# A new hand-fixed issue order, with landing constants and a port rule in its planner, for an adaLN block of linear attention and SwiGLU

## The chip, the cores and the metric

One core of one Trainium2 chip runs the kernel. The metric is the device time of one execution in microseconds (us), the median of the runs shown; lower is better. The core has five instruction streams: TensorE (PE, matrix products; its weight loads are listed apart as PEld and overlap), VectorE (DVE), ScalarE (ACT), GpSimd (POOL) and SyncE (SP, which here issues nearly all DMAs). Each engine takes its instructions strictly in the order in which the program lists them, and waits on semaphores for results of the others.

## The reference

```python
# x: 2048 x 512; H = 32 heads of 16; F = 1376; c: 1 x 512
mod = silu(c) @ w_mod                      # sa, ca, ga, sb, cb, gb, 512 each
h = layernorm(x) * (1 + ca) + sa
q, k, v = h @ wqkv                         # per head
phi(t) = concat(softmax(t @ w_phi), softmax(-t @ w_phi))
kv = sum_s phi(k)^T v ;  z = sum_s phi(k)
o = phi(q) kv / (phi(q) z + 1e-6)
x = x + ga * (o @ wo)
h = layernorm(x) * (1 + cb) + sb
x = x + gb * ((silu(h @ w_gate) * (h @ w_up)) @ w_down)
```

## The kernel before

The 2048 tokens are 16 tiles of 128, in four chunks of four. The work is not issued as it is written down. Every step (one matmul group, one evacuation, one DMA) is registered with `pl.op` together with what it reads and writes, and, where several engines can do it, with one alternative for each (L390 to L400 for a normalization: DVE, ACT or POOL). The table `ORDER` (L46) then fixes the order: entry `x` is operation `x // 4` in the order of registration, done by alternative `x % 4`. `Plan.run` (L168) walks the table once, gives each operation a planned start from fixed durations and constants, and emits the instructions sorted by that start. Two steps of one engine therefore come in the order in which the table has them, whatever the constants say. The constants decide three things beside the order: which buffer slot a tile gets, how steps of different engines interleave in the listing, and how many filler matmuls (`fill`, L1037 on, instructions at L1054, on a tile of ones) go in front of a PE step whose planned start lies after the end of the one before. Before the first kv step the filler takes the whole planned gap, later about 85% of it, and none after 90 us of the plan.

An alternative marked `DVE*` is a VectorE step that the planner believes to take the SBUF port that VectorE and GpSimd share. Nothing in the program enforces that: there is no semaphore for it, it only moves planned starts.

Stages, in the order of time, with the lines at which they show in the profile:

- Loads, all on SP's queue (L289): x of chunk 0, `Wk2`, `w_phi`, the two modulation parts of `w_mod` in three pieces, x of chunk 1 in two, then x of chunk 2, `Wq2`, `wv_sb`, x of chunk 3.
- `w_phi` is folded into the key and query weights (`fold_phi`): four blocks i, each transposed (PE at L519 for the keys, DMA at L292 for the queries), evacuated (L523), multiplied with a block-diagonal matrix `BD` (L502, product at L530) and evacuated again (L533, L534).
- Modulation: `silu(c)` times `w_mod`, four groups k (PE L473), evacuated as `modA` (DVE L478).
- First layernorm (`first_norm`): bn_stats (L348), bn_aggr (L349), rstd (POOL L381 and L382, or ACT L377 and L378), negative mean (L384), normalization (L392, L396 or L398). Transposes of the result are PE's for tiles 0 to 5 (L563, L414), evacuated with the modulation (L566, L567, L422), and DMAs for tiles 6 to 15 (L577), modulated at L585 to L589.
- `k_tile` i: K (PE L619), its two exponentials (ACT L634), V (PE L623), sums (DVE L640), their reciprocals (ACT L644, L645), `va` (DVE L650), two POOL steps (L648, L657). `kv_tile` (PE L663) accumulates. `q_tile` (PE L686, ACT L690, DVE L694, POOL or DVE L701, DMA L705) is the same for the queries. These share six PSUM banks (`one_ps`).
- `gate`, `mod_cols` and `spread_gate` make the other modulation vectors from two further loads of `w_mod`.
- `prepare`: attention output (PE L824), transposed (L843 or a DMA, L847), projected (PE L857), added to x, second layernorm, transposed again (L414 or a DMA, L871).
- Feed-forward: `ffn_gu` (PE L909; ACT L916; DVE L919, or ACT L923 and POOL L925), `ffn_tail` (PE L955), `ffn_down` (PE L987; DVE L997 and DVE or POOL L1001, or DVE L993), stores (L1007). Only the last token tile is stored in three pieces of columns: 0 to 256, 256 to 384 and 384 to 512.

## Time and profile before

| | us |
|---|---|
| median of 3 runs | 199.46 (199.35 to 200.03) |
| span of the profiled execution, first to last instruction | 197.6 |
| PE busy in the span | 192.9 |
| DVE, ACT, POOL busy | 139.9, 111.6, 119.5 |
| mean granted PE clock of the span | 1.000, so the 2.4 GHz level |

The record gives the profiled execution's span, not a device time of its own; the median of the runs is 1.9 us longer than the span. In the rows below a timeline row is "start, duration of the group, engine, line, operation, out<-in, count"; a group of xN instructions is merged, and its duration runs from the first start to the last end, so that steps that overlap in the pipeline are closer together than their single durations. A row of five windows gives for each engine the busy time and the number of instructions in that stretch. A DMA row ends with the median time from issue to landing.

### The profile page before, as it was taken

The page shows a single profiled execution, that of the slowest core. Times are in us where ns is not written, and L with a number is a line of the kernel's source. Part 1 is how long each engine was busy: PE and PEld are TensorE (multiplying, and loading weights), DVE is VectorE, ACT ScalarE, POOL GpSimd, SP SyncE. Part 2 cuts the span into 40 slices and gives each one's busy share as a digit, 9 for nine tenths or more (in the row PEclk, how much of TensorE's full clock was granted, in tenths as well). Part 3 has the DMA queues.
Part 4 walks back from the last instruction along what each step waited for, and adds up shares of the span by engine and source line. Part 5 has one row for each costly group of instructions (what it writes and reads, how often), then busy time and mean ns, then how long its engine had stood idle before and what let it go on. Part 6 is the DMA issues. An engine that isn't in the chain of part 4 may idle for free.

```text
span 197.6 us, 4084 instructions
## 1 busy us (share of the span) xinstructions
PE 192.9 (98%) x1495; PEld 108.4 (55%) x1495; DVE 139.9 (71%) x272; ACT 111.6 (56%) x252; POOL 119.5 (60%) x198
## 2 busy tenths in 40 slices
PE   7999999999999999999999999999999999999993
PEld 2765555555754776886575554454445444444452
DVE  5999999999999999989868689384122421181653
ACT  2699999999769982665263625435723411235200
POOL 1459999999996669656757979406761004065310
PEclk9999999999999999999999999999999999999999
DMA  6997994999928672835377515400340020100202
GB/s 210 370 373 116 168 316 162 213 181 389 324 53 170 117 138 42 157 65 102 77 113 135 109 36 87 100 0 0 80 98 25 0 63 17 56 15 27 80 29 79
DMA packets 51142, 24.17 MB, mean 122 GB/s; under 512 B 42449, under 2 KB 47922, under 8 KB 51122
## 3 DMA queue, kind: packets, MB, share of 16 engines
q1 hardware_dynamic: 50976, 23.88, 50.0%
q8 instruction: 11, 0.18, 0.3%
q14 instruction: 9, 0.07, 0.1%
q10 hardware_dynamic: 146, 0.03, 0.1%
HBM read 11.58 MB, written 2.10 MB: 69 GB/s over the span
## 4 chain that ended last, share of the span: by engine, by line
PE 98%; DVE 0%; issue 0%
PE one_ps L909 35%; PE one_ps L987 19%; PE one_ps L857 7%; PE one_ps L623 7%; PE one_ps L619 7%; PE one_ps L686 7%; PE kv_ps L1054 4%; PE one_ps L955 3%; PE kv_ps L663 2%; PE kv_ps L824 2%; PE one_ps L530 1%; PE one_ps L473 1%; PE one_ps L414 1%; PE one_ps L519 0%; PE one_ps L722 0%; DVE ones L296 0%
## 5 line engine op out<-in xcount | busy, mean ns | idle before, releaser
L909 PE MATMUL one_ps<-hT,wgu_sb 128*128 128x512 bf16 (+2 forms) x480 | 75.7, 308 | 0.0
L909 PEld LDWEIGHTS <-wgu_sb 128*128 128x128 bf16 x480 | 40.3, 98 | 27.7
L916 ACT ACTIVATE sg<-one_ps 128x512 bf16<-128x512 f32 (+1 forms) x41 | 23.7, 588 | 41.8 <-PE one_ps L909 29.9
L925 POOL TENSOR_TENSOR gu<-usb,sg 128x512 bf16<-128x512 bf16 x19 | 21.8, 1151 | 39.7 <-ACT usb L923 19.9
L987 PE MATMUL one_ps<-wd_sb,gu 128*128 128x512 bf16 (+1 forms) x160 | 37.7, 372 | 0.0
L919 DVE TENSOR_TENSOR gu<-one_ps,sg 128x512 bf16<-128x512 f32 (+1 forms) x22 | 14.3, 652 | 21.1 <-PE one_ps L909 19.0
L987 PEld LDWEIGHTS <-gu 128*128 128x128 bf16 x180 | 16.6, 98 | 16.7
L997 DVE TENSOR_TENSOR fg<-one_ps,gab 128x512 bf16<-128x512 f32 (+1 forms) x16 | 10.5, 669 | 19.6 <-PE one_ps L987 19.4
L348 DVE BATCH_NORM_STATS2 st<-x_c 128x6 f32<-128x512 bf16 x32 | 21.0, 679 | 0.1
L640 DVE TENSOR_REDUCE S<-e 128x64 f32<-128x1024 bf16 x16 | 19.1, 1207 | 0.2
L694 DVE TENSOR_REDUCE Sq<-eq 128x64 f32<-128x1024 bf16 x16 | 19.0, 1201 | 0.0
L923 ACT CAST usb<-one_ps 128x512 bf16<-128x512 f32 x19 | 11.3, 594 | 13.5 <-PE one_ps L909 13.2
L690 ACT ACTIVATE eq<-one_ps 128x512 bf16<-128x512 f32 x32 | 17.3, 644 | 2.2 <-PE one_ps L686 2.2
L634 ACT ACTIVATE e<-one_ps 128x512 bf16<-128x512 f32 x32 | 16.9, 600 | 0.0
L657 POOL TENSOR_TENSOR e<-e,S 128x512 bf16<-128x512 bf16 x16 | 16.8, 1056 | 0.1
L857 PE MATMUL one_ps<-wo_sb,oT 128*128 128x512 bf16 x64 | 16.1, 379 | 0.0
L623 PE MATMUL one_ps<-wv,hT 128*128 128x512 bf16 x64 | 16.1, 379 | 0.0
L619 PE MATMUL one_ps<-wk,hT 128*128 128x512 bf16 x64 | 15.8, 379 | 0.0
L686 PE MATMUL one_ps<-wq,hT 128*128 128x512 bf16 x64 | 15.8, 379 | 0.0
L701 POOL TENSOR_TENSOR eq<-eq,Rq 128x512 bf16<-128x512 bf16 x13 | 14.2, 1096 | 0.5
L860 DVE TENSOR_TENSOR x_c<-x_c,one_ps 128x512 bf16<-128x512 bf16 x16 | 10.6, 674 | 4.5 <-PE one_ps L857 4.4
L880 ACT ACTIVATE hT<-raw,modB 128x256 bf16<-128x256 bf16 x16 | 8.9, 594 | 8.1 <-DMA raw<-xn 8.1
(120 smaller groups left out, 279.8 us busy)
## 6 DMA issues: line engine op xcount, KB each, us to landing
wmod_sb<-in_w_mod_dram SPq DMA_DIRECT2D x2, 1024.0 KB, 8.5
out_dram<-ot SPq DMA_DIRECT2D x15, 128.0 KB, 2.0
x_c<-in_A_x_dram SPq DMA_DIRECT2D x3, 512.0 KB, 6.7
wgu_sb<-in_B_w_up_dram SPq DMA_DIRECT2D x1, 1376.0 KB, 10.2
wgu_sb<-in_B_w_gate_dram SPq DMA_DIRECT2D x1, 1376.0 KB, 13.1
wd_sb<-in_B_w_down_dram SPq DMA_DIRECT2D x1, 1280.0 KB, 6.8
wk<-in_A_wqkv_dram SPq DMA_DIRECT2D x1, 512.0 KB, 4.9
wmod_sb<-in_w_mod_dram SPq DMA_DIRECT2D x1, 512.0 KB, 5.3
```

Of the source, the lines that this page charges most:

```text
L348: pl.op("DVE", r=reads, w=[st6], us=0.6, fn=lambda: nc.vector.bn_stats(st6()[:], src))
L619: nc.tensor.matmul(pk()[:], lhsT=hT[c_i][k][:, cols], rhs=Wk2[:, k, :], start=(k == 0), stop=(k == KD - 1))
L623: nc.tensor.matmul(v()[:], lhsT=hT[c_i][k][:, cols], rhs=wv_sb[:, k, :], start=(k == 0), stop=(k == KD - 1))
L640: pl.op("DVE", r=[e], w=[Ss], us=1.13, fn=lambda: nc.vector.tensor_reduce(Ss()[:].rearrange("p g s h -> p (g s h)"), e()[:].rearrange("p g ...
L686: nc.tensor.matmul(pq()[:], lhsT=hT[c_i][k][:, cols], rhs=Wq2[:, k, :], start=(k == 0), stop=(k == KD - 1))
L690: pl.op("ACT", r=[pq, btab], w=[be[sg]], us=0.48, fn=lambda sg=sg: nc.scalar.activation(eq[:, :, sg].rearrange("p g h f -> p g (h f)"), pq ...
L694: pl.op("DVE", r=be, w=[Sq], us=1.13, fn=lambda: nc.vector.tensor_reduce(Sq()[:].rearrange("p g s h -> p (g s h)"), eq[:].rearrange("p g s ...
L857: nc.tensor.matmul(a()[:], lhsT=oT()[:, j0 + j, :], rhs=wo_sb[:, j, :], start=(j == 0), stop=(j == KD - 1))
L909: nc.tensor.matmul(ps_()[0:fsz, q * n:(q + 1) * n], lhsT=wgu_sb[:, k, i, m * P:m * P + fsz], rhs=h2[k], start=(k == 0), stop=(k == KD - 1))
L916: pl.op("ACT", r=[g, btab], w=[sg], us=0.08 + 0.41 * L / CW, fn=lambda: nc.scalar.activation(sg()[0:fsz, 0:L], g()[0:fsz, 0:L], ACT.Silu))
L925: pl.op("POOL", r=[usb, sg], w=[gu], us=0.17 + 0.98 * L / CW, fn=lambda: nc.gpsimd.tensor_tensor(gu()[0:fsz, 0:L], usb()[0:fsz, 0:L], sg() ...
L987: nc.tensor.matmul(fp()[:], lhsT=b()[0:fsz, c0:c0 + P], rhs=wd_[0:fsz, m, wcs], start=(m == 0), stop=(m == FM - 1))
```

## The change

The table `ORDER` is replaced: the same 995 operations in another order, 59 of them by another engine. Planner constants change: the time that a DMA transpose takes to land after its transfer falls from 1.1 to 0.6, the sizes that stand for the load times of the first twelve loads are set anew, and the rule for `DVE*` becomes one over intervals: a `DVE*` step is no longer put behind all POOL steps that the table lists before it, but only out of the way of the POOL intervals that it would overlap (and POOL steps out of the way of `DVE*` ones). The source order of the loads of x chunk 2, `Wq2`, `wv_sb` and x chunk 3 changes, and with it their operation numbers; in both tables SP issues them in the order x 2, `Wq2`, `wv_sb`, x 3. Of the last tile, the piece of columns 256 to 384 is now stored on ACT's queue and that of 384 to 512 on SP's; the new order also computes 384 to 512 before 256 to 384, so that the piece finished last is on ACT's queue in both kernels.

```diff
 ORDER = [
-    0, 48, 4, 188, 8, 52, 12, 16, 20, 24, 56, 80, 60, 72, 220, 84, 76, 156, 228, 192, 64, 204, 89, 172, 232, 224, 92, 160, 196, 164, 177, 102, 201,
...
+    48, 0, 4, 8, 52, 56, 80, 188, 68, 60, 192, 72, 12, 16, 20, 84, 172, 76, 89, 156, 24, 220, 204, 28, 32, 176, 228, 36, 40, 224, 208, 44, 232,
...
 ]
-    DMA = (1.7, 385e3, 0.5, 0.6, 1.15, 1.1)
+    DMA = (1.7, 385e3, 0.5, 0.6, 1.15, 0.6)
...
+        held = {"POOL": [], "DVE*": []}
...
-            if o.alt[0] == "DVE*":
-                o.start = max(o.start, free["POOL"])
...
+            star = o.alt[0] == "DVE*"
+            if star or o.eng == "POOL":
+                for s, e in held["POOL" if star else "DVE*"][-8:]:
+                    if o.start < e and o.start + o.alt[1] > s:
+                        o.start = e
...
-            if o.alt[0] == "DVE*":
-                free["POOL"] = max(free["POOL"], o.end)
+            if star or o.eng == "POOL":
+                held[o.alt[0]].append((o.start, o.end))
...
-    later(x_ch[0][:], x_v[0], bx[0:4], 400)
-    later(Wk2[:], wqkv_v[:, :, D:2 * D], bwk[0:1], 690)
+    later(x_ch[0][:], x_v[0], bx[0:4], 440)
+    later(Wk2[:], wqkv_v[:, :, D:2 * D], bwk[0:1], 755)
...
-    for k, n, kb in ((0, 2, 770), (2, 1, 280), (3, 1, 280)):
+    for k, n, kb in ((0, 2, 470), (2, 1, 262), (3, 1, 250)):
...
-            on_act = c1 == D and h == 1
+            on_act = c0 == D // 2 and c1 < D
```

Decoded, the first steps of PE stand in this order (k: modulation group; fold i: block i of the key weights, or of the query weights where it says so; T: transposes of normalized tiles; K, V, q: tiles):

| before | after |
|---|---|
| transposes of Wk 2, w_phi, transposes of Wk 0, 3, 1 | transposes of Wk 2, w_phi, transposes of Wk 1, 0, 3 |
| fold 2, fold 0, k 0, fold 1, k 1, fold 3 | k 0, k 1, fold 2, fold 0, fold 1, k 2, k 3 |
| T of tiles 0 and 1 (one of four), k 2, k 3, T of tiles 2 and 3 (half), T of 0 and 1 (three), T of 2 and 3 (half) | T of tiles 0 and 1 (four), fold 3, T of tiles 2 and 3 (both halves) |
| K 0, K 1, K 2, T of 4 and 5 (half), K 3, T (half), V 1, V 0 | K 1 and K 0 (halves in turn), K 2, K 3, V 0, T of 4 and 5, V 1 |
| K 4, V 4, K 5, query folds 1, 0, V 5, query fold 3, V 3, query fold 2, V 2, kv 0, q 0, kv 1, q 2 | query fold 2, V 2, query fold 3, V 3, query fold 1, K 4, query fold 0, K 5, q 3, q 0, kv 0, kv 1, q 2 |

Beside them: DVE takes bn_stats and bn_aggr of tiles 0 and 1 before the statistics of tiles 2 and 3 (before: bn_stats of tile 2 in between), then `BD` after the first negative mean. POOL does the constant masks (L329 to L332) first instead of after three normalizations, and normalizes all of tiles 0 to 3 (before: tiles 1 and 2, with ACT for 0 and DVE for 3) and makes the rstd of chunk 2 (before: ACT). ACT evacuates all four T of tiles 0 and 1 (before: three, DVE one) and fold 3 after them. SP's order becomes: query-weight transposes 2, 1, 3, 0 (before 3, 1, 0, 2); transposes of tiles 6 and 7; the first further load of `w_mod` (before: after those of tiles 8 to 11 and the load of `w_down`); transposes of tiles 8 to 11; the second further load of `w_mod` and `wo`; transposes of tiles 12 to 15; `w_down`, `w_up`, the rest of `w_down`, `w_gate`; and only then the first `pT` (before: the first `pT` ahead of `w_up` and `w_gate`). At the end PE does tiles 14, 15 (0 to 256) and 12 in another interleaving, then tile 13 and the two last pieces, as before.

## Rows read from the trace of the kernel before

**Rows 1.** The page, busy time of each engine in the span:
```profile
PE 192.9 (98%) x1495; PEld 108.4 (55%) x1495; DVE 139.9 (71%) x272; ACT 111.6 (56%) x252; POOL 119.5 (60%) x198
```
**Rows 2.** Timeline of PE, 9.9 to 17 us (columns as told above):
```profile
9.90 0.54 PE L473 MATMUL one_ps<-silucT,wmod_sb 128*128 128x1 bf16 x16
...
11.37 1.54 PE L1054 MATMUL kv_ps<-ones 128*128 128x512 bf16 x7
12.74 2.75 PE L619 MATMUL one_ps<-wk,hT 128*128 128x512 bf16 x12
15.33 0.48 PE L1054 MATMUL kv_ps<-ones 128*128 128x512 bf16 x2
...
16.96 1.89 PE L623 MATMUL one_ps<-wv,hT 128*128 128x512 bf16 x8
```
**Rows 3.** Timeline of PE around two of its later waits:
```profile
46.06 1.03 PE L623 MATMUL one_ps<-wv,hT 128*128 128x512 bf16 x4
47.02 0.17 PE L471 MATMUL one_ps<-zero_one,ones 1*128 1x8 bf16 x1
...
62.56 1.89 PE L686 MATMUL one_ps<-wq,hT 128*128 128x512 bf16 x8
64.44 0.29 PE L414 MATMUL one_ps<-ident_b,xn 128*128 128x128 bf16 x2
```
**Rows 4.** Busy time in stretches: PE, PEld, DVE, ACT, POOL, then clock, DMA share, GB/s:
```profile
25.00:30.00 5.00, 5.00 (x36) 2.42 (x33) 5.00 (x10) 4.90 (x16) 5.00 (x8) 1.00 1.00 334
...
50.00:55.00 5.00, 5.00 (x80) 3.28 (x79) 4.86 (x9) 3.04 (x10) 5.00 (x8) 1.00 0.78 267
```
**Rows 5.** Timeline of DVE, 4 to 10.7 us:
```profile
4.33 1.87 DVE L348 BATCH_NORM_STATS2 st<-x_c 128x6 f32<-128x512 bf16 x3
6.12 0.23 DVE L349 BATCH_NORM_AGGREGATE ln_mv<-st 128x2 f32<-128x6 f32 x2
...
7.01 0.69 DVE L502 TENSOR_TENSOR BD<-one_ps,bm 128x512 bf16<-128x512 f32 x1
...
10.48 0.17 DVE L478 COPY modA<-one_ps 128x8 f32<-128x8 f32 x1 [0.38 <-PE one_ps L473]
```
**Rows 6.** Timeline of POOL and ACT in the first 16 us, and POOL's group at L657:
```profile
6.76 0.72 POOL L382 TENSOR_TENSOR ln_mv<-ln_var,mhalf 128x2 f32<-128x2 f32 x1
...
13.72 1.52 POOL L398 TENSOR_SCALAR xn<-x_c,ln_mv,ln_nmr 128x512 bf16<-128x512 bf16 x2 [0.54 <-DVE ln_nmr L384]
...
10.68 1.68 ACT L566 ACTIVATE hT<-one_ps,modA 128x256 bf16<-128x256 bf16 x3
...
L657 POOL TENSOR_TENSOR e<-e,S 128x512 bf16<-128x512 bf16 x16 | 16.8, 1056 | 0.1
```
**Rows 7.** SP's issues in time, and DMA issues of 0 to 30 us by landing:
```profile
2.19 1.44 SPq L289 DMA_DIRECT2D wmod_sb<-in_w_mod_dram  x3
...
wmod_sb<-in_w_mod_dram SPq DMA_DIRECT2D x2, 256.0 KB, 5.6
...
13.06 5.89 SPq L292 DMA_TRANSPOSE WT<-wq  x4
...
raw<-xn SPq DMA_TRANSPOSE x3, 3.3
```
**Rows 8.** Landing of L292's transposes, and DMA issues of 30 to 44 us:
```profile
DMA to landing us min/median/max: 2.5/2.6/4.2
...
pT<-eq SPq DMA_TRANSPOSE x1, 5.7
```
**Rows 9.** The last matmul, and the last store (issues of 190 us on):
```profile
194.12 0.22 PE L987 MATMUL one_ps<-wdg,gut 96*128 96x128 bf16 x1
...
out_dram<-ot ACTq DMA_DIRECT2D x1, 32.0 KB, 1.9
```
**Rows 10.** Instructions of L1001: count, then ns min/median/max, first and last start:
```profile
L1001 DVE TENSOR_TENSOR ot<-x_c,fg x11: 411/424/1104, 109.3 to 194.0; 128x512 bf16<-128x512 bf16 x11
L1001 POOL TENSOR_TENSOR ot<-x_c,fg x5: 667/1154/1729, 124.6 to 191.0; 128x512 bf16<-128x512 bf16 x4, 128x256 bf16<-128x256 bf16 x1
```

More of the change, by code (lines that the diff above doesn't have):

```diff
@@ L428, in modulate_T @@
               r=[tp, bmod], w=[b[2 * jp + jj] for b in [bdst] + list(also) for jj in range(2)])
-    later(x_ch[0][:], x_v[0], bx[0:4], 400)
-    later(Wk2[:], wqkv_v[:, :, D:2 * D], bwk[0:1], 690)
-    later(wphi_sb[:], A_w_phi.rearrange("h (q t) f -> (h q) (t f)", t=4), [bphi], 70)
-    for k, n, kb in ((0, 2, 770), (2, 1, 280), (3, 1, 280)):
+    later(x_ch[0][:], x_v[0], bx[0:4], 440)
+    later(Wk2[:], wqkv_v[:, :, D:2 * D], bwk[0:1], 755)
+    later(wphi_sb[:], A_w_phi.rearrange("h (q t) f -> (h q) (t f)", t=4), [bphi], 75)
+    for k, n, kb in ((0, 2, 470), (2, 1, 262), (3, 1, 250)):
         later(wmod_sb[:, k:k + n, 0:2 * D], wmod_v[:, k:k + n, 0:2 * D], bm1[k:k + n], kb)
     for t in (0, 2):
-        later(x_ch[1][:, t:t + 2, :], x_v[1][:, t:t + 2, :], bx[TPC + t:TPC + t + 2], 270)
-    later(wv_sb[:], wqkv_v[:, :, 2 * D:3 * D], [bwv], 560)
-    later(Wq2[:], wqkv_v[:, :, 0:D], bwq[0:1], 570)
-    for c_i in (2, 3):
-        later(x_ch[c_i][:], x_v[c_i], bx[c_i * TPC:(c_i + 1) * TPC], 620)
+        later(x_ch[1][:, t:t + 2, :], x_v[1][:, t:t + 2, :], bx[TPC + t:TPC + t + 2], 256)
+    for c_i, kb in ((2, 520), (3, 620)):
+        if c_i == 3:
+            later(Wq2[:], wqkv_v[:, :, 0:D], bwq[0:1], 570)
+            later(wv_sb[:], wqkv_v[:, :, 2 * D:3 * D], [bwv], 550)
+        later(x_ch[c_i][:], x_v[c_i], bx[c_i * TPC:(c_i + 1) * TPC], kb)
     sig = const.tile([P, KD], FP32, name="sig")
```

79 rows, old and new, of the table ORDER are left out of this document.

## The prediction

> **What bounds the kernel now.** I read the busy times first: PE 192.9 of 197.6 us [rows 1]. Some of that is filler, so the next view is PE's timeline, and in it the distance from one start to the next. Twelve K matmuls start at 12.74 and the next group at 15.33 [rows 2]: 2.59 / 12 = 0.216 us each, though one is listed much longer. Smaller ones, from the same timeline of which group 2 shows a part: 0.055 us for 128 columns, 0.025 for a modulation column. Laying these distances along all PE steps of the kernel, those from the first K matmul on sum to 180.0 us. The last starts at 194.12 [rows 9], so 12.74 + 180.0 = 192.8, and only 1.4 us between 12.74 and 194.2 is not work: 0.32 filler at 15.33 [rows 2], 0.10 before 47.02 (46.06 + 4 x 0.216 = 46.92) [rows 3], about 0.15 before 64.44 by the same sum [rows 3], the rest smaller. The change takes no PE work away. It can gain before 12.74, in this 1.4 us, and in the 3.4 us from the last matmul to the end, and lose anywhere else. In the middle that is easy: DVE, ACT and POOL are at 4.90 to 5.00 of 5 us at 25 to 30 us, while ACT has air at 50 to 55 (3.04) [rows 4].
>
> **The start, walked by hand.** I follow the new order with distances of before; from one engine's end to another's start I put 0.1 to 0.2 us (POOL's pow ends 7.48 and DVE and POOL go on within that).
>
> DVE: before, the aggregates of tiles 0 and 1 stand behind a third bn_stats, at 6.12 [rows 5]. Three take 1.87, one 0.68, so they are 0.60 apart; behind two the aggregates end near 5.8. POOL's pow then ends near 6.9 instead of 7.48 (6.76 + 0.72 [rows 6]). Two further bn_stats fit into that wait. The price is `BD`: behind the first negative mean it ends near 7.8 instead of 7.70 [rows 5].
>
> POOL normalizes all four tiles, 0.75 apart (two in 1.52 [rows 6]): from 7.3, tiles 0 and 1 end at 8.8; tiles 2 and 3, whose mean comes at 9.2, at 10.8. The masks that go first cost nothing: POOL is idle then until the statistics come.
>
> `modA`: the third `w_mod` piece is issued last of three that begin at 2.19 and take 1.44, so near 3.2, and lands 5.6 later [rows 7]: 8.8. Before, its products waited at 9.90 [rows 2] behind transposes that waited for normalized tiles, and `modA` came at 10.48 [rows 5]. In the new order they stand behind three folds that end at 8.8; two groups of eight at 0.025 end at 9.2, and `modA` comes at 9.4: 1.0 us sooner.
>
> ACT then evacuates four transposes, 0.45 to 0.55 apart (three in 1.68 with a short wait among them [rows 6]), 9.7 to 11.6, and fold 3, to 12.1. PE makes the transposes of tiles 2 and 3 ahead of the first K matmul: 10.9 to 11.36. So K 1 and K 0 start at 11.36; their second halves wait for fold 3, 12.3, and they end at 13.15. Before: 12.74 + 8 x 0.216 = 14.47. **Gain 1.3.**
>
> K 2, K 3, V 0 and the transposes of tiles 4 and 5 follow (normalized by 15.6), V 1 starts at 16.2. Before it starts at 16.96 [rows 2], and V 0 (0.86) is behind it: **gain 1.6**, the filler at 15.33 among it.
>
> Then some is given back. The query-weight transposes wait for the load of `Wq2`, whose place on SP is unchanged: they start at 13.06 in any order [rows 7] and land after 4.2 for the first and 2.5 to 2.6 for later ones [rows 8], that is at 17.2, 17.7, 18.8 and about 20. The new order puts a query fold right behind V 1, at 17.1: wait 0.2. The next, after V 2, takes the transpose issued third: it is wanted at 18.4 and there at 18.9: wait 0.5. q 3 then waits some 0.15 for the evacuation of the last query fold, and starts at 22.3. Counted in PE work done, that is 1.6 - 0.85, **about 0.7 us ahead** of before (the walk's error is some 0.3 either way).
>
> **The middle.** From 22.3 the sum of PE distances puts K 9 at 33.8 and kv 15 at 53.2, where before has it at 53.1 with one query tile (0.86) less done. I take the middle as neutral, 0, by three views:
> - POOL, from its first step of chunk 1 at 14.07: eight normalizations of 0.75, rstd of chunk 2 at 1.2, five small and five large kv steps (1.06 long, 1.02 apart [rows 6]), two part and four full modulations, and a wait of 0.35 for the reciprocal of tile 0: its last modulation for K 9 ends near 33.5. It fits with 0.2 to 0.3 to spare. Moving rstd of chunk 2 to POOL costs it 1.2 us and gives ACT 0.5.
> - The waits before 47.02 and 64.44 may go or come back elsewhere. The first is for the second `w_mod` load, moved ahead by some 13 us, and I count up to -0.1 for it. The transposes at 64.44 now have 5.1 us after the first projection instead of 5.8: between -0.15 and +0.7. Both ends stay in the range.
> - The 59 moved alternatives shift a net three operations to POOL (DVE one less, ACT two less), less than 2 us in 112 to 140 [rows 1]. Behind 100 us these engines have air, and I cost it at 0; without that air it would be at most that 2 us.
>
> **The port rule** costs and gives nothing on PE's path by itself: it emits no wait, it moves planned starts. What it lets happen shows in before: an addition at L1001 takes DVE 424 ns in the median and 1104 at worst, POOL 1154 and 1729 [rows 10]. So overlapped pairs pay 0.6 to 0.7 us each, where neither engine was on PE's path. The Trainium skill, "SBUF — State Buffer", section "SBUF: two separate sides", calls this port pair an exclusive lock that the later instruction waits for in full; the maxima fit that, and each new overlap would then cost the loser at most one POOL instruction. As PE has work queued there, the sum stays as it is.
>
> **The stores**: 0. Renamed pieces, same sizes, same queues in the same order of finishing. The ACT store lands 1.9 us after issue [rows 9]; the end follows PE's last matmul as before, 3.4 us behind.
>
> **Sum.** Span 197.6 - 0.7 = 196.9; with the 1.9 us outside the span, **198.76**.
>
> **The rivals.**
> - *The start is kept, and the old waits go too.* -0.7 with up to another 0.5 off: 198.2 to 198.7. Part of the forecast's case.
> - *The supply engines take the gain back.* At 25 to 30 us all three are full [rows 4]; a PE that is ahead only waits there for a bank or for POOL. If POOL's tail at 33.5 slips by 0.5 to 1, K 9 and kv 4 stand still by 0.3 to 0.8: 199.0 to 199.6, most likely 199.2. For it: the margin of 0.2 to 0.3. Against: ACT's air at 50 to 55 shows that before had some slack to give.
> - *Transposes land late behind a load* (slower). The first further `w_mod` load, 1 MB, goes ahead of the transposes of tiles 8 to 11. Without such a load ahead, three `raw` transposes land in 3.3 us [rows 7]; the first `pT`, issued behind the 512 KB of `wo`, takes 5.7 [rows 8]. If the second transpose of the pair, issued near 24.5, takes 5.7 instead of 3.3, it lands at 30.2 instead of 27.8; POOL stands still before its modulations, and K 9 and kv 4 lose 2.4 - 0.25 = 2.1. That gives 199.46 - 0.7 + 2.1 = 200.9. It decides from a landing after about 28.8. Against: that pair is issued some 4 us after the load, long enough for most of it. The Trainium skill, "DMA: Bandwidth & Descriptors", section "Two DMAs through the same engine are not ordered", says that descriptors of one queue start in order, which would make transposes stand behind any load issued before them; the 5.7 us fits.
> - *The change does nothing at the start*, because filler placed by the plan holds PE until the old time, or ACT's four evacuations (one more than before) do. 199.4.
>
> **How the numbers follow.** Forecast with its better variant 0.49, from 198.0 to 198.9. Supply engines 0.25, 199.0 to 199.6. Late landings 0.18, from 199.7 (half a microsecond late) to 201. Nothing 0.08, 199.3 to 199.6. A measurement tells about 0.3%, 0.6 us, from no change, so faster means under 198.86: nearly all of the first case and a little of the second, 0.49. Same, to 200.06: 0.35. Slower: 0.16. The range 198.0 to 200.2 leaves out the larger part of the late landings and a little below.
>
> **What would show it.** Right: first K matmul at 11.2 to 11.6, fold 3's evacuation the last thing before the second halves, two short PE waits at 17 to 19, q 3 at 22.0 to 22.6, no filler at 15.33, K 9 within 0.3 of 33.8. Supply: gaps of PE at 25 to 50 ended by POOL or ACT evacuations. Late landing: K 9 or kv 4 after 35, POOL idle before L589. Wrong throughout: a first K matmul after 12.3, or PE waits in the feed-forward part after 66 us, where I counted none.

## The result: slower, and where the time lies in the profile after

The changed kernel takes 202.23 us (median of 6, 201.40 to 204.85) against 199.68 (199.35 to 200.26) for the kernel before on the same chip: ratio 1.0124, 95% interval 1.0086 to 1.0162. That is slower by 2.5 us where 0.7 less was forecast, and outside the range. An execution more than 1.5% above the fastest of its kernel counts as slow and stands in the medians and ranges but in no ratio: here that of 204.85 us (without it the median is 201.58), further on two of the four of `wmod_half` (206.39 and the profiled 204.99) and one of `after_delay` (209.61). The profiled execution is one of 203.66 us with a span of 201.8.

Its page, busy time of each engine (before: [rows 1]):

```profile
PE 192.4 (95%) x1469; PEld 107.9 (53%) x1492; DVE 137.8 (68%) x272; ACT 110.9 (55%) x248; POOL 121.4 (60%) x202
```

PE does the same work in a span that is 4.2 us longer. So PE stands still, and the view to read is the list of its waits between 30 and 110 us (waiting line <- what ended the wait: us in total, times, longest us):

```profile
PE kv_ps L669 <- POOL e L663: 1.2, 1, 1.2
PE one_ps L961 <- DVE x_c L866: 0.8, 1, 0.8
PE kv_ps L830 <- DMA pT<-eq: 0.5, 1, 0.5
PE one_ps L961 <- POOL hT L888: 0.3, 1, 0.3
PE kv_ps L830 <- DVE st L353: 0.2, 1, 0.2
```

The same view of the kernel before, in a second profile of it, has no line at all. (This view counts a wait from the modelled end of the matmul before it; by the start-to-start sum of the prediction each is about 0.15 longer, and so I give them from here on.) The lines of the changed kernel stand some 6 below (L663 of before is L669 here, L824 is L830, L955 is L961).

In time, for the profiled execution: 1.36 us before kv 4 at 34.44; 0.38 at 64.34 and 0.31 at 66.89; 0.94 and 0.49 at 79.95 and 80.52; 0.67 at 107.26: 4.15 in all. Before has 0.10 at 47 and 0.33 at 64 and 70. Two names in the list are only the last releaser that the view found: the matmuls at 64.34 use the `pT` issued at 61.01, whose landing is not in the trace, and those at 79.95 and 80.52 use `hT`, which ACT and POOL began to make when the `raw` transpose landed at 79.27.

The start, as a timeline of PE, DVE and POOL in the changed kernel (start, duration, engine, line; the brackets are the idle time ahead and what ended it); before: [rows 2, 5, 6].

```profile
8.64 0.55 PE L479 MATMUL one_ps<-silucT,wmod_sb 128*128 128x1 bf16 x16 [0.33 <-DMA wmod_sb<-in_w_mod_dram]
9.05 0.38 PE L536 MATMUL one_ps<-BD,WT 128*128 128x128 bf16 x4
...
9.78 0.54 PE L479 MATMUL one_ps<-silucT,wmod_sb 128*128 128x1 bf16 x16
...
9.53 0.69 DVE L540 CAST wk<-one_ps 128x512 bf16<-128x512 f32 x1 [1.07 <-ACT ln_mv L383]
10.14 0.15 DVE L389 TENSOR_REDUCE ln_nmr<-ln_mv 128x2 f32<-128x4 f32 x1
...
10.38 1.53 POOL L403 TENSOR_SCALAR xn<-x_c,ln_mv,ln_nmr 128x512 bf16<-128x512 bf16 x2 [1.51 <-DVE ln_nmr L389]
...
11.99 0.61 PE L419 MATMUL one_ps<-ident_b,xn 128*128 128x128 bf16 x8
12.43 3.62 PE L625 MATMUL one_ps<-wk,hT 128*128 128x512 bf16 x16
```

The reader sees one chain without a gap: the first `w_mod` piece lands at 8.59, PE does its products, behind them in PE's order stands a fold, DVE casts the fold, behind that cast in DVE's order stands the negative mean of tiles 2 and 3, POOL normalizes them, PE transposes them, and the first K starts at 12.43. (The bracket of DVE's cast names ACT's L383, but that had ended at 9.17; the fold's products begin at 9.05 and end at 9.43.) The forecast had 11.36.

### The profile page after: what moved, and what is told of

The parts are those of the page before. It is cut to its first block, busy times and chain, and to the rows that moved or that the text cites. A ratio compares the mean times of both kernels' runs of the same rounds, so it can differ in the third digit from the quotient of the medians.

```text
span 201.8 us, 4048 instructions
## 1 busy us (share of the span) xinstructions
PE 192.4 (95%) x1469; PEld 107.9 (53%) x1492; DVE 137.8 (68%) x272; ACT 110.9 (55%) x248; POOL 121.4 (60%) x202
## 4 chain that ended last, share of the span: by engine, by line
PE 63%; DMA 14%; POOL 8%; DVE 5%; ACT 4%; issue 3%; SPq 1%; POOLq 0%; DVEq 0%; ACTq 0%
PE one_ps L915 27%; PE one_ps L993 15%; DMA raw<-xn 8%; PE one_ps L863 4%; PE one_ps L625 3%; PE one_ps L692 3%; PE one_ps L629 3%; DMA wmod_sb<-in_w_mod_dram 3%; POOL xn L403 2%; DMA pT<-eq 2%; PE one_ps L961 2%; ACT e L640 2%; DVE st L353 2%; PE kv_ps L669 2%; POOL ln_rstd L365 1%
## 5 line engine op out<-in xcount | busy, mean ns | idle before, releaser
L915 PE MATMUL one_ps<-hT,wgu_sb 128*128 128x512 bf16 (+2 forms) x474 | 74.2, 307 | 0.3
L993 PE MATMUL one_ps<-wd_sb,gu 128*128 128x512 bf16 (+1 forms) x154 | 36.5, 372 | 0.3
L1003 DVE TENSOR_TENSOR fg<-one_ps,gab 128x512 bf16<-128x512 f32 (+1 forms) x16 | 10.7, 666 | 14.5 <-PE one_ps L993 14.5
L707 POOL TENSOR_TENSOR eq<-eq,Rq 128x512 bf16<-128x512 bf16 x16 | 16.9, 1058 | 0.8
L663 POOL TENSOR_TENSOR e<-e,S 128x512 bf16<-128x512 bf16 x16 | 17.0, 1065 | 0.7
L863 PE MATMUL one_ps<-wo_sb,oT 128*128 128x512 bf16 x62 | 15.5, 379 | 0.1
L629 PE MATMUL one_ps<-wv,hT 128*128 128x512 bf16 x60 | 15.4, 379 | 0.2
L692 PE MATMUL one_ps<-wq,hT 128*128 128x512 bf16 x61 | 15.3, 379 | 0.2
L886 ACT ACTIVATE hT<-raw,modB 128x256 bf16<-128x256 bf16 x15 | 8.3, 594 | 7.5 <-DMA raw<-xn 7.5
```

What stands on the lines that cost most here:

```text
L629: nc.tensor.matmul(v()[:], lhsT=hT[c_i][k][:, cols], rhs=wv_sb[:, k, :], start=(k == 0), stop=(k == KD - 1))
L692: nc.tensor.matmul(pq()[:], lhsT=hT[c_i][k][:, cols], rhs=Wq2[:, k, :], start=(k == 0), stop=(k == KD - 1))
L863: nc.tensor.matmul(a()[:], lhsT=oT()[:, j0 + j, :], rhs=wo_sb[:, j, :], start=(j == 0), stop=(j == KD - 1))
L915: nc.tensor.matmul(ps_()[0:fsz, q * n:(q + 1) * n], lhsT=wgu_sb[:, k, i, m * P:m * P + fsz], rhs=h2[k], start=(k == 0), stop=(k == KD - 1))
L993: nc.tensor.matmul(fp()[:], lhsT=b()[0:fsz, c0:c0 + P], rhs=wd_[0:fsz, m, wcs], start=(m == 0), stop=(m == FM - 1))
```

## The experiments

All times are medians, with the ratio to runs of the kernel before on the same chip (199.5 to 199.8) and its 95% interval behind them. "Waits" are PE's, by start-to-start sums.

**1. Both kernels once more, and each half of the order alone.** `ORDER` is one list, so the first part of one can be joined to the rest of the other: the entries of the first up to about 52 to 55 us, then all others in the sequence of the second (`old` is the table of before, numbered for the changed kernel).

```diff
 # tail_of_before: the changed kernel with
+ORDER = new[:370] + [x for x in old if x // 4 not in {y // 4 for y in new[:370]}]
-            on_act = c0 == D // 2 and c1 < D
+            on_act = c1 == D and h == 1
 # head_of_before: the changed kernel with
+ORDER = old[:350] + [x for x in new if x // 4 not in {y // 4 for y in old[:350]}]
```

> The changed kernel once more, for its spread and for a second trace. Theory 'late transposes' (the w_mod load ahead of the transposes of tiles 8 to 11 makes them land late): those two land 5.5 to 7 us after issue again, PE waits 1.2 to 1.6 us near 33 us, time 201.4 to 203.7 with most of the spread from later waits. Theory 'second half' (the loss is made behind 60 us): the wait near 33 differs from run to run, those behind 60 us stay at 2 to 3 us. Theory 'loads' (the first loads land at other times in each execution, and the new order has no margin for it): the first w_mod piece lands anywhere between 7.5 and 8.6 us, and the time follows it, 201.4 with the early, 203.5 with the late landing.

> The kernel before once more, for a second trace. Theories 'late transposes' and 'second half': 199.4 to 200.2, PE waits of 1.4 us in all from 12.7 us on, first w_mod piece at 7.5 us. Theory 'loads': the first w_mod piece lands at another time than 7.5 (up to 8.6) here too, and the time still stays within 0.5 us of 199.7, since this order plans with later landings.

> The first 370 entries of the new ORDER (the work to about 55 us), then the remaining operations in the old order and with the old engines; constants of the new planner, old queues of the last two stores. Theory 'late transposes': the wait near 33 us stays, time 201 to 202. Theory 'second half': the waits behind 60 us go, time 199.7 to 200.2 (the seam costs up to 0.5). Theory 'loads': as the changed kernel when the first loads are late, 201 to 202.5, else near 200.

> The first 350 entries of the old ORDER (the work to about 52 us), then the remaining operations in the new order; constants of the new planner and new queues of the last two stores. Theory 'late transposes': no wait over 0.5 us before 50 us, time 199.7 to 200.7 (the seam costs up to 0.8). Theory 'second half': the waits behind 60 us stay at 2 us or more, time 201.5 or more. Theory 'loads': near 200.3 in all runs, little spread.

Measured: after_again 202.28 (ratio 1.0141, 1.0120 to 1.0163), before_again 199.46 (0.9996), tail_of_before 201.64 (1.0127, 1.0082 to 1.0172), head_of_before 201.62 (1.0089, 1.0063 to 1.0116). Both halves lose. In the first half (tail_of_before) it is the wait before kv 4, 1.07, and a wait of 1.12 for `wv`, which landed at 16.74 in that execution, not at 14.46 as in the first profile of before. In the second half (head_of_before) it is the waits at 78.3 and 78.9 (0.87, 0.49), behind a `raw` transpose of 72.65 that took 5.0 us, and at 105.5 (0.59), with 0.70 of filler and of waiting for POOL's normalization at the seam. 'Second half' had the waits of the changed kernel's tail stay at 2 to 3 us; in after_again they are 1.69. Its wait near 33, 0.39, is also under the 1.2 to 1.6 of 'late transposes', and its first `w_mod` piece, at 9.28, came later than 'loads' had it. Waits in the second profile of the changed kernel:

```profile
PE kv_ps L830 <- DMA pT<-eq: 0.9, 2, 0.6
PE kv_ps L669 <- POOL e L663: 0.2, 1, 0.2
```

Those at 80 us are not there; the `raw` transpose behind them, issued at 74.24 and 74.10, landed after 5.0 us in the first profile and after 3.2 in the second.

**2. The load ahead of the transposes, halved.**

```diff
-        cols = slice((2 + 2 * i) * D, (4 + 2 * i) * D)
+        cols = slice((2 + i) * D, (3 + 3 * i) * D)
```

> The changed kernel in its own order, with the first of the two further w_mod loads cut to its first 512 columns (0.5 MB in place of 1 MB) and the other 512 put into the second (1.5 MB), so that half as much stands in the queue ahead of the transposes of tiles 8 to 11. 'Late transposes': the transpose issued near 22.5 lands at about 28 in place of 29.4 to 29.7 (5.5 us after issue in place of 6.5 to 7), the wait ahead of kv 4 (0.39 to 1.36 us in three runs) falls to between 0 and 0.3; the second load lands up to 1 us later, which can bring a wait of 0 to 0.7 at the mod B columns near 34.5. Time 0.3 to 1 us below the changed kernel's on the same chip's scale, 200.8 to 202. If the load isn't the cause: landing and wait as before, 201.4 to 203.7.

Measured: 203.80 (201.36 to 206.39), ratio 1.0121 (1.0072 to 1.0171). The DMA issues of 20 to 27 us in the changed kernel (KB each, median us to landing), then what hangs on them, POOL's and PE's timeline:

```profile
wmod_sb<-in_w_mod_dram SPq DMA_DIRECT2D x2, 1024.0 KB, 6.4
raw<-xn SPq DMA_TRANSPOSE x3, 5.5
...
31.08 2.28 POOL L595 TENSOR_SCALAR hT<-raw,modA 128x512 bf16<-128x512 bf16 x3 [1.52 <-DMA raw<-xn]
...
34.44 0.43 PE L669 MATMUL kv_ps<-va,e 128*128 128x68 bf16 x8 [1.20 <-POOL e L663]
```

The two transposes behind the load took 7.0 and 5.5 us and landed at 29.39 and 30.92 (before: 3.3 [rows 7]). POOL stood still 1.52 us for the second, and its kv step came late for PE. With half the load, issues of 20 to 28.5 us and PE's waits of 30 to 60 us:

```profile
wmod_sb<-in_w_mod_dram SPq DMA_DIRECT2D x1, 512.0 KB, 4.1
raw<-xn SPq DMA_TRANSPOSE x3, 3.6
...
PE one_ps L479 <- DMA wmod_sb<-in_w_mod_dram: 0.9, 1, 0.9
```

The first transpose behind the half load took 3.1 us, the second 3.6, and the wait before kv 4 is gone. In its place PE waits 0.94 for the second load, now 1.5 MB: that the load is the cause of the late landings is shown; the time is not won, for the load is wanted elsewhere. (The range was to 0.7 for this second wait; the miss is in its size. The two executions at full clock took 201.36 and 202.61; of the profiled one's clock more is said at the end.)

**3. TensorE's code loads.** In the DMA view a packet of queue 8, kind "instruction", 0.02 MB, comes once per about 128 matmuls (11 of 16 KB in the changed kernel). After the `raw` transpose was issued at 74.24 in the changed kernel such a packet began at 77.05. Issues of 74 to 75 us, and packets of 76.5 to 77.5 (packets, MB, share of 16 engines):

```profile
raw<-xn SPq DMA_TRANSPOSE x1, 5.0
...
q8 instruction: 1, 0.02, 7.2%
```

If these packets hold up transposes, then matmuls added at the very start, where PE only turns over filler, shift the packets against the order and move the late landings with them. So: the same filler in smaller pieces.

```diff
 # after_code32
-                fns.append(lambda n=min(left, CW): f(n))
-                left -= CW
+                fns.append(lambda n=min(left, P): f(n))
+                left -= P
 # after_code77 and before_code78: this, and the first gap filled with
+            if t0 < 3.0:
+                fns += [lambda: nc.tensor.matmul(kv_ps[:, 0, 0:1], lhsT=ones[0:1, 0:P], rhs=ones[0:1, 0:1],
+                                                 start=True, stop=True, skip_group_check=True)] * 60
+                left = 0
```

> The changed kernel with its first filler matmuls cut into pieces of 128 columns: the same columns, some 32 matmuls more before the first K, none elsewhere, so that TensorE's code loads (one 16 KB packet of queue 8 after every 128 or so matmuls) come some 32 matmuls sooner in the program. In the run after_again they start at 27.3, 37.8, 54.0, 68.3, 76.8, 90.5 and 103.2 us. 'Code loads' (a transpose issued 1 to 2.9 us ahead of such a packet lands 4 to 5 us after its issue in place of 3.0 to 3.4): the packets move to about 25, 35, 50.6, 64, 73.4, 87.4 and 100.5; the transpose raw issued at 74.1 lands in 3.0 to 3.4 us whatever the run, the pT ones issued at 88.3 and 101.0 too (4.5 and 4.6 before), and those issued near 62.2, 71.4, 85.2, 97.9 and 99.3 become the late ones. Waits near 80 us 0, near 106 us under 0.2, new ones of up to 1 us behind the late ones. Time 201 to 202.5. 'Second half' (the order itself asks for its transposes too late, wherever the code loads fall): the same late landings at 88.3 and 101.0 and the same wait of 0.6 to 0.8 near 106; time 201.5 to 203.7.

> As after_code32, with some 77 matmuls more before the first K (the first four fillers are replaced by 60 of one column each). 'Code loads': the packets move to about 20, 32, 45, 58.6, 71.2, 83.5 and 95; late become the Wq transposes issued near 17.4 and 18.7, and the pT, gut ones issued near 57.3, 70.1, 81.2 and 82.6; the transposes issued near 35, 74, 88, 98 and 101 land in 3.0 to 3.5 us, and the waits near 80 and 106 us are gone (1.43 and 0.67 in the profile of the changed kernel, 0 and 0.76 in its second one). The transposes of tiles 8 to 11 stay late for the w_mod load. Time 200.5 to 202. 'Second half': waits near 106 stay at 0.6 to 0.8; time 201.5 to 203.7.

> The kernel before with some 78 matmuls more ahead of the first K, as in after_code77. In before_again the packets of queue 8 start at 28.8, 40.8, 53.6, 65.8, 75.4, 88.6 and 101.1 and only the pT transpose issued at 99.9 is late (4.3 us). 'Code loads': the packets move to about 21, 34.4, 48, 58, 69, 81 and 93; late become the transposes issued near 19.1, 33.2, 67.3 (oT, on which TensorE waits 0.2 us at 70.7 already: that wait becomes 0.8 to 2), 78.4 or 79.8, 89.9 and 91.3; time 200 to 201.5, 0.5 to 2 us slower than before although no step of the order is moved. 'Second half': nothing changes but the start, 199.3 to 199.9.

Measured: after_code32 203.49 (1.0205, 1.0162 to 1.0248), after_code77 202.52 (1.0157, 1.0123 to 1.0191), before_code78 200.42 (1.0032, 1.0008 to 1.0055). The first two are above what 'code loads' allowed (202.5 and 202); the landings decide. In after_code77 packets begin near 70.9, 83.1 and 94.6. The `raw` transpose of 74.9 lands after 3.1 us, the `pT` of 67.9 and 80.6 after 4.9 and 5.5; issues of 74 to 76 and of 67.8 to 69.5 us, and PE's waits of 30 to 130:

```profile
raw<-xn SPq DMA_TRANSPOSE x1, 3.1
...
pT<-eq SPq DMA_TRANSPOSE x2, 4.7
...
PE kv_ps L830 <- DMA pT<-eq: 2.1, 2, 1.2
PE kv_ps L830 <- DVE st L353: 0.2, 1, 0.2
```

The waits at 80 and 106 are gone, and new ones stand at 72.9 (1.06) and 86.2 (1.35), each behind a late `pT`. The kernel before can be hurt in the same way: in before_code78 a packet begins near 107.1, the `oT` transpose of 105.3 lands after 4.6 us, and its projection waits. Issues of 105 to 106, packets of 106.8 to 107.8, timeline of PE:

```profile
oT<-o SPq DMA_TRANSPOSE x1, 4.6
...
q8 instruction: 1, 0.02, 5.5%
...
109.94 1.04 PE L857 MATMUL one_ps<-wo_sb,oT 128*128 128x512 bf16 x4 [0.36 <-DMA oT<-o]
```

(0.52 by start-to-start; the other 1.1 us of its longer span is its first K, 13.68, behind the cut filler.) The wait that I had expected at 70.7 did not come: the packet was at 68.9 and the `oT` issued at 67.7 took 4.1 us, but the wait there stayed 0.26. In after_code32 one wait is left behind 55 us that is longer than 0.1, 2.02 at 68.0, for a `pT` that was issued at 62.97 and used at 67.95, 4.98 us later (packet near 65.9; its landing is not in the trace); none stands near 80 or 106. It lost 3 us at the start as well (see the clock, at the end).

Over 16 profiles (all but the two of the failed re-laying in 5), 418 transposes are issued between 55.5 and 127 us with a known landing. Of the 53 issued 0.75 to 2.75 us ahead of such a packet, 39 took 4 us or more (median 4.3, most 5.6); of the 288 with no packet from 0.6 us before to 3.3 us after their issue, none did (median 3.15, most 3.94). after_again's `raw` of 74.10 is one of those that passed, 2.7 us ahead of its packet; the changed kernel's of 74.24, 2.8 ahead, just outside the first group, is one of those that did not. In these profiles no transpose of that stretch took 4 us without a packet that began from its issue to 3.05 us after it. Theory 'code loads' stands; whether TensorE waits then depends on how long after the usual landing the order puts the first use.

**4. How much room the two orders leave.** A small DMA from the same source goes ahead of each `pT`, `oT` and `raw` transpose, so that each is issued later (the edit of `pT`; `oT` and `raw` likewise).

```diff
+    def late(src, dst, srcs):
+        turns.append(0)
+        nc.sync.dma_start(scr[len(turns) % 8][0:1, :], src)
+        nc.sync.dma_start(dst, srcs, transpose=True)
-        pl.op("XBAR", r=be, w=[pT], us=1.4, fn=lambda: nc.sync.dma_start(
-            pT()[:], eq[:].rearrange("p g s h f -> p (g s h f)"), transpose=True))
+        pl.op("XBAR", r=be, w=[pT], us=1.4, fn=lambda: late(
+            eq[0:1, 0, 1, 0, :], pT()[:], eq[:].rearrange("p g s h f -> p (g s h f)")))
```

> The kernel before, with a DMA of 32 bytes from the same source put into SP's queue right ahead of every transpose of pT, oT and raw (some 45 of them, from 37 us on), so that each is issued later by what such a DMA takes SP, an estimated 0.4 to 0.5 us from the 0.4 to 0.57 us of SP's plain loads. Nothing else is changed. 'No reserve' (the order of before leaves each transpose about 0.5 us between its usual landing and its use, for its plan reckons 1.1 us behind the transfer where the new one reckons 0.6; the new order leaves nearly none, so code loads of 1 to 2 us and other lateness go straight into TensorE): the delay is mostly taken by the reserve; TensorE waits behind 55 us rise from 0.4 to at most 1.2 us, 199.7 to 200.5. 'Equal reserve': the same loss as in after_delay within 0.5 us.

> The changed kernel with the same 32-byte DMA ahead of each transpose of pT, oT and raw. 'No reserve': every place where the order lets TensorE use a transpose as it lands (kv near 64 and 106, the output projection near 67, the gate and up matmuls near 80) grows by 0.3 to 0.5 us and others join: waits behind 55 us rise by 1.5 to 4 us, 203.5 to 206.5. 'Equal reserve': the rise over the changed kernel's 202.2 is that of before_delay over before within 0.5 us.

Measured: before_delay 202.65 (1.0148, 1.0132 to 1.0164), after_delay 207.96 (1.0383, 1.0342 to 1.0423). The added DMAs, 30 and not 45, take SP 0.51 to 0.61 us each. Before loses 2.9 us; the changed kernel, at ratios of 1.0383 against 1.0124 and 1.0141, loses 4.8 to 5.2 (5.7 by the medians). 'Equal reserve' misses by some 2 us. 'No reserve' has the sign, but both losses are above its ranges, and before had less room than I gave it (at most 1.2 us of waits was expected): transposes that follow each other add their delays on SP. PE's waits, before_delay:

```profile
PE one_ps L865 <- DMA oT<-o: 1.3, 2, 1.0
PE one_ps L865 <- ACT sg L924: 1.1, 1, 1.1
```

and after_delay (two waits, at 81.19 and 81.75, stand in the changed kernel without the delay as well, 0.94 and 0.49, where `raw` is late):

```profile
PE one_ps L871 <- DMA oT<-o: 2.5, 2, 1.4
PE one_ps L969 <- ACT hT L894: 1.2, 1, 1.2
PE kv_ps L838 <- DVE ln L362: 1.1, 1, 1.1
PE kv_ps L838 <- DMA pT<-eq: 0.9, 2, 0.7
PE kv_ps L677 <- POOL e L671: 0.7, 1, 0.7
PE one_ps L969 <- POOL hT L896: 0.3, 1, 0.3
```

**5. Orders laid again with room.** Steps were shifted on all engines by the kernel's own durations until transposes land earlier ahead of their use. The table `ORDER` is all that differs (and, in the first two, the load amounts of before).

> The issue order of the changed kernel with steps shifted on all engines (some 150 of TensorE's 290 steps a little out of their old places, and VectorE's, ScalarE's and GpSimd's to match) so that each transpose has, by the kernel's own durations, 0.5 us and more between its usual landing and its first use, that it bears a few transposes 1.4 us late, and that the third w_mod piece may land at 9.7 us (the mean of the profiles so far: 8.85 to 10.9) in place of 8.8; the amounts of the load model in the plan are those of the kernel before, for that is where they lead. 'No reserve': the waits behind 60 us fall from 1.7 to 2.8 us to under 0.8, no wait of the 0.6 us at 105; the time falls by 1.5 to 2.5 us to 199.4 to 200.8. If it isn't the missing reserve (the new arrangement itself, or its use of GpSimd, costs the time): 201.3 to 203.

> The same treatment of the order of the kernel before (numbered as in the changed kernel, with its rule for the port and its store queues). 'No reserve': TensorE's waits behind 55 us stay at 0.2 to 0.8 us, as before's 0.4; the first K stays near 12.3 to 12.6 us; 198.8 to 199.9, at most 0.4% from before, since before's order has 0.7 us of waits to give and its start hangs on the w_mod landing. Rival, 'the changed parts harm' (port rule and store queues kept from the change): 200.3 to 201.5.

Measured: after_relaid 209.25 (1.0495), before_relaid 206.99 (1.0375): both far off. PE's waits behind 55 us did fall, to about 1.0 and to 0.10, and the last matmul of before_relaid starts at 194.13, as in before; but its end is 10.1 us later, not 3.4. My re-laying had looked at PE's end alone and left the last additions behind the buffers of earlier stores. POOL's timeline in before_relaid:

```profile
193.01 1.78 POOL L1006 TENSOR_TENSOR ot<-x_c,fg 128x512 bf16<-128x512 bf16 x2 [1.65 <-DVE fg L1002]
200.22 1.15 POOL L1006 TENSOR_TENSOR ot<-x_c,fg 128x512 bf16<-128x512 bf16 x1 [5.43 <-DMA out_dram<-ot]
```

So these times say nothing on the reserve. Two more, shifted only behind 52 us and with the end watched: behind the new start, and behind the old one.

> The issue order of the changed kernel, unchanged up to about 52 us (its first 330 entries); behind that steps of all engines are shifted a little (113 of TensorE's 290 stand out of their old places) so that transposes land earlier ahead of their first use, and so that the last stores leave as early as before. 'No reserve': the start and the wait ahead of kv 4 are as in the changed kernel; TensorE's waits behind 55 us fall from 1.7 to 2.8 us to 0.2 to 1.0; the time behind the last matmul stays 3.4 to 3.5 us; 200.2 to 201.5. Rival 'what the change did behind 52 us costs its time in another way than by landings' (engine choice, port rule, store queues, all kept): 201.5 to 203.

> head_of_before (the old order up to about 52 us, the new one behind, new rules and store queues throughout; 201.6 us) with the part behind 52 us shifted in the same way. 'No reserve': TensorE's waits and fillers behind 55 us fall from 2.8 us to 0.1 to 0.7, as in the kernel before (0.35 to 0.4); first K at 12.5 to 12.7; the time is that of before, 198.9 to 199.9. Rival: 200.5 to 201.8.

Measured: after_reserve 201.70 (1.0112, 1.0074 to 1.0150), head_reserve 200.90 (1.0063, 1.0042 to 1.0085). In after_reserve one wait of 0.19 and 1.09 of filler and of waiting for POOL's normalization at 65.8 are left behind 55 us, and its profiled execution, 200.83, has the end 3.45 behind the last matmul. But its six times lie in two groups, 200.6 to 201.2 and 202.2 to 203.0; three of six are over what 'no reserve' allowed, and two of these three have a mean granted clock of 0.992. The ratio is not clear of the changed kernel's 1.0124: that the waits go with the room is shown, that the time does is not. head_reserve is 0.7 under head_of_before (the intervals overlap) and still 1.4 over before: 0.56 and 0.51 of waits, and a first K at 14.14, for the first `w_mod` piece came at 10.0 in that execution. Two more runs: the same kernel again, and what all these variants share, the new constants, rules and store queues, with the old order:

```diff
 # order_old: the changed kernel with
-ORDER = new
+ORDER = old   # the two renumbered loads mapped
```

> Everything of the change but its order: the old issue order (numbered for the new kernel) under the new constants, the new port rule and the new store queues. 'The order alone' (start chain and landings): as before, 199.2 to 199.9, waits behind 55 us 0.3 to 0.6. Rival 'the constants and queues take part' (fewer or more filler matmuls, the swapped queues of the last stores): 200.2 to 201.5.

> head_reserve once more, for a second look: in its profile the third w_mod piece landed at 11.31 us, the latest of all, and the first K came at 14.14. 'Loads' (the start hangs on that landing, which changes from execution to execution): with a landing below 10 the first K comes at 12.5 to 12.7 and the execution takes 199.2 to 200.3; the median as before, 200.5 to 201. If the first K stays at 14 with an early landing, the order of the start is to blame and the times all stay above 200.5.

Measured: order_old 200.41 (1.0047, 1.0023 to 1.0070), head_reserve2 200.36 (1.0048, 1.0027 to 1.0069). For order_old the rival is right, by 0.9 us, and the trace says by what: its last matmul starts at 194.30, as early as before's within 0.3, and the end is 4.20 behind it, not 3.45. Its stores of 193 us on (KB, us to landing), then those of the changed kernel from 196 on:

```profile
out_dram<-ot SPq DMA_DIRECT2D x1, 128.0 KB, 2.3
out_dram<-ot ACTq DMA_DIRECT2D x1, 32.0 KB, 1.5
out_dram<-ot SPq DMA_DIRECT2D x1, 32.0 KB, 2.5
```

```profile
out_dram<-ot SPq DMA_DIRECT2D x1, 128.0 KB, 1.9
out_dram<-ot SPq DMA_DIRECT2D x1, 32.0 KB, 1.5
out_dram<-ot ACTq DMA_DIRECT2D x1, 32.0 KB, 1.9
```

With the old order the swapped rule puts the piece that is finished first on ACT and the last two on SP, one behind the other: 0.75 us. The swap belongs to the new order and is worth nothing in itself. The rest of the change without its order costs 0.1 to 0.2, within what a measurement can tell. So the loss comes with the order.

head_reserve2 had its piece at 8.28, and the first K still came at 13.14, not at 12.5 to 12.7: the expectation 'loads' missed. In PE's timeline planned filler stands right ahead of it; what made this start later than before's is not settled:

```profile
11.84 1.46 PE L1059 MATMUL kv_ps<-ones 128*128 128x512 bf16 x6
13.14 1.24 PE L624 MATMUL one_ps<-wk,hT 128*128 128x512 bf16 x5
```

With waits of 0.59, 0.43 and 0.12 behind 100 us and this start the profiled execution, 200.85, is 1.3 us over before. No variant is faster than the kernel before.

## Why the prediction was wrong, point by point

- **The landing of `w_mod`** is the step of the start that failed. Up to tiles 0 and 1 the walk held: POOL's pow was to end near 6.9 and ended at 6.97; they were to be normalized by 8.8 and were at 8.87. But the mean of tiles 2 and 3, put at 9.2 with no load in its chain, came at 10.14, for it stands behind the cast of a fold that stands behind the first `w_mod` piece, and that piece landed at 7.51 in the one profile that I read and at 8.59 in the changed kernel's. The new chain holds its length: piece to first K is 8.59 to 12.43, 9.28 to 13.12, 8.36 to 12.21 (tail_of_before), 8.05 to 11.86 (after_code77), 8.43 to 12.28 (after_reserve): 3.81 to 3.85 each time (after_delay, 7.78 to 11.84, is 4.06). From 7.51, earlier than any landing measured under the new order, that would give 11.35, an estimate; that the forecast said 11.36 is luck, for its walk did not have this chain. The old start does not follow the piece like that: before_again has it at 8.35, later by 0.8 than the first profile, and a first K at 12.54, earlier by 0.2:

```profile
11.17 1.54 PE L1054 MATMUL kv_ps<-ones 128*128 128x512 bf16 x7
12.54 0.81 PE L619 MATMUL one_ps<-wk,hT 128*128 128x512 bf16 x3
```

  At the same landing of 8.35 the new start is worth 12.54 - 12.21 = 0.33, not 1.3. `wv` and `Wq2` vary too (`wv` 14.5 to 16.8). V 1 came at 17.30, not 16.2, and q 3 at 23.03, not 22.3. Why these landings change from execution to execution no run here settles.
- What hid this: I had all products of `w_mod` behind three folds. Those of the first piece stand ahead of them, those of the other two behind. The third piece lands 1.3 us behind the first in nearly all profiles, so a chain from either gives the same time; after_delay tells them apart. There the third came 1.55 behind the first, at 9.33, PE waited for it, and the first K came 2.51 behind it, as in the other five (2.53 to 2.56):

```profile
8.97 0.76 PE L487 MATMUL one_ps<-silucT,wmod_sb 128*128 128x1 bf16 x16
...
11.84 1.46 PE L633 MATMUL one_ps<-wk,hT 128*128 128x512 bf16 x6
```

  So the start hangs on both pieces, on the third where it comes later than 1.3 us behind the first.
- **Late transposes behind the load** was a rival at 0.18, with 2.1 us, deciding from a landing after 28.8. They landed at 29.4 and 30.9 (29.5 and 30.4 in the second profile); PE lost 1.36, 0.39 and 1.07 in three profiles, 0.49 in after_reserve, 0.83 in after_delay and 0.19 in after_code77. The mechanism is right; the price was 0.7 to 1.9 too high, the chance too low, and the sign, kv 4 after 35, was set too late (34.44). The argument against it, that the pair is issued 4 us after the load, compared with the wrong end: the load issued at 21.0 lands at 27.05, and the pair was issued at 22.4 and 25.4. The rule of the Trainium skill, "DMA: Bandwidth & Descriptors", section "Two DMAs through the same engine are not ordered", that descriptors of a queue start in order, agrees with the 7.0 us, and with 3.1 once the load was half as long.
- **Behind 66 us "I counted none"** was named as what would prove the prediction wrong throughout, and it did: 1.2 to 2.4 us of waits behind 66 us, 1.7 to 2.8 behind 60. The step that failed is the pricing of everything behind 55 us by the busy shares of DVE, ACT and POOL, with 0 for the landings of transposes. All but 0.2 to 0.3 us of these waits end at DMA transposes, directly or through the step that reads one, and SP's queue was never walked there. The line that speaks of it stood in the change: the plan's allowance from transfer to landing falls from 1.1 to 0.6 us. 0.6 fits the usual landing of 3.2 us; 1.1 held half a microsecond for one that lands later, and in each kernel here some land 1 to 2 us later. Shown is that the new order has less room (2.9 against some 5 us lost to the same delay) and that TensorE's code loads make the late landings. The traces have the room itself: from the issue of the fourth to tenth `pT` to the first matmul that uses it pass 3.7 to 8.6 us in before_again and 3.3 to 4.6 in after_again (k-th transpose to k-th group of eight `kv_ps<-KVZ,pT`). The constant by itself does not make the difference: order_old has the 0.6 and 3.6 to 8.4 us. It is the order that takes the room away; whether it was laid out under the smaller constant the record does not say.
- **Port rule and moved alternatives**, 0: nothing of the loss is traced to them. order_old, which has the rule, loses only what its stores lose; the alternatives were not tried alone. **The stores**, 0: right, the end is 3.45 to 3.5 behind the last matmul in both kernels; order_old shows what the price would be without the order that goes with them.
- **The sum.** after_again against before_again, PE only, span + 2.84: up to 20 us + 0.4 (the first K 0.58 later, 0.14 less filler behind it), from 20 to 60 us + 0.7, behind 60 us 1.69 of waits and 0.21 of filler against 0.40, so + 1.5: 2.6. The other 0.2 are gaps too small to name. In the first profile the last part is + 2.6, for the `raw` transpose of 74.24 came late there.

## What to carry to other kernels

A landing read from one execution is a sample: take it from several, and ask of a new order not how early it is with the earliest one but how it moves with a late one. When an order is replaced, compare the time from the issue of each transfer to its first use, by walking the queue that issues the transfers to the end of the kernel, and price every use that comes as the transfer usually lands. A gain at the start, here 0.7 us in the forecast, is lost again where later transfers arrive just in time.

## What the runs showed of the hardware that I had not expected

- A 16 KB packet of TensorE's code, once per about 128 matmuls, came with a longer landing of most DMA transposes issued 0.75 to 2.75 us ahead of it (median 4.3 us in place of 3.15, at most 5.6; 14 of 53 stayed under 4), and some 78 matmuls more at the start of a program change which transposes that hits 60 to 100 us later.
- The same loads in the same order on the same queue land up to 2.5 us apart from profile to profile (first `w_mod` piece 7.5 to 10.0 us), and 1.7 apart in two profiles of one kernel (head_reserve and head_reserve2, 10.0 and 8.28).
- In after_code32 a late start also costs clock. Busy time of PE, PEld, DVE, ACT, POOL, then granted clock, DMA share, GB/s:

```profile
7.00:8.50 1.50, 0.42 (x17) 0.42 (x17) 0.15 (x2) 0.00 (x0) 1.25 (x2) 1.00 1.00 376
...
10.00:12.00 2.00, 2.00 (x40) 2.00 (x40) 0.76 (x2) 1.15 (x5) 0.14 (x1) 0.50 1.03 392
12.00:14.00 2.00, 2.00 (x29) 2.00 (x27) 1.69 (x4) 1.98 (x6) 1.38 (x2) 0.50 1.12 359
```

  `w_phi` came at 8.04 there (5.8 to 6.4 in most), PE was busy 0.42 of the 1.5 us ahead of 8.5, and from 8.85 to 15.7 us the granted clock is 0.5, the 1.2 GHz level: the first K starts at 16.04, 5.1 behind the third `w_mod` piece in place of 2.53. `wmod_half` has the same from 8.44 to 11.85, with `w_phi` at 7.91 and a mean granted clock of 0.991. On record, 10 of the 40 executions with the new start (the re-laid order left out) have a mean granted clock of 0.992 or less; of the 144 with the old start (the kernel before's own among them) none is under 0.995. So this loss comes with the new start, and it is part of the wide spread (201.4 to 204.9 against 199.0 to 200.3): the longest execution has 0.992. It is not all of it, as the next, 203.66, has 0.999. Why the old start is spared was not tried; the old order has the same steps ahead of `w_phi`, and in none of its profiles does `w_phi` land later than 7.0.
